# Row gathers two experts ahead, two of four turns at the beginning of a choice, and no drains on GpSimd, in an attention and mixture-of-experts kernel

## The chip, the cores and the metric

The kernel runs on one core of a Trainium2 chip. The metric is the device time of one execution in microseconds (us). TensorE (PE in the profile) multiplies matrices, VectorE (DVE) and ScalarE (ACT) work on elements, GpSimd (POOL) here issues the transfers that go by lists of rows, and SyncE (SP) issues plain transfers.

## The reference

Windowed attention over four batches of eight heads gives 3072 tokens of 512 numbers; then every token goes to one of eight experts.

```python
x = attention(q, k, v, n_global, n_local)          # (3072, 512)
logits = normed(x) @ normed(expert_emb).T / tau    # (3072, 8)
expert_idx = np.argmax(logits, axis=1)
gate_w = softmax(logits)[arange, expert_idx]
for e in range(8):
    mask = expert_idx == e
    h = np.maximum(x[mask] @ w1[e], 0.0)           # w1: (8, 512, 1024)
    out[mask] = gate_w[mask, None] * (h @ w2[e])   # w2: (8, 1024, 512)
```

## The kernel before

Up to about 200 us the kernel computes the attention, writes its rows to `x_dram` in main memory, and lists the tokens of each expert. From there on it goes through the eight experts, one after the other; the change is in this part alone.

**Rows of an expert.** Up to 512 tokens of an expert are fetched as four tiles of 128 rows. From expert 2 on each tile comes in four gathers of a quarter of a row (`gather_quarters`, gather L1030), sixteen in all, in an order that lets VectorE alone turn the tile (`turn_squares`, L1039) to have the 512 numbers of a token along the partitions. Every two gathers, a small copy on GpSimd (L1029) waits until the gathers four places before have landed, so that not too many are under way. The tiles come from a pool of eight buffers, so two experts' rows have a place.

**A choice.** The number of tokens of an expert is known only at run time. `expert` has a `tc.Switch` (L1415) with an arm for each width (256, 288, ... 512 tokens); TensorE, ScalarE and VectorE branch into the arm of that width, and out of it again. The branches are under L1825 in the profile, and the first instruction of an arm is a prefetch hint under L1415. GpSimd and SyncE have no work in the arms.

**In an arm** (`first_by_seven`) the first layer is done in seven products of half size (L1347) instead of eight, by sums of blocks: TensorE puts products into banks, VectorE adds a bank to the hidden tile (`plus`, L1357), and further products are added onto the same banks when `plus` has read them. The order is: product into x, product into y, x again, y again, v, y, v. The first `plus` reads y, ahead of the second product into y, which is the fourth of all. Between them, `fill()` lets VectorE do other small work out of the list `spare`: sums of the second layer's weights (L1090 to L1093) and of the next expert's first weights (L1115 to L1118).

**After the choice** VectorE finishes the last part of the expert before (L1165), turns the four tiles of the next expert, and sums them (`token_sums`, L1090 to L1093 on `xsum` and `xT`). In its order among them are the sums of the second layer's seven products (`Pair.begin` and `Pair.end`, L1153 on TensorE; u2 and u3 are L1158). ScalarE scales u2 (L1183) and u3 (L1190) and then p5 (L1206); TensorE's last product of the expert, added onto the bank that L1206 reads, waits for L1206.

**GpSimd's order** in the loop over experts: in iteration e it issues the gathers for expert e+1 (`prepare`), then the scatters of expert e-1's results to the output (L1300), then a drain (L1795). SyncE loads the next expert's weights: w1 in four loads of 512 KB (L169), w2 in one of 2 MB (L170), each as soon as the expert that used the buffer before is done with it. All orders on the engines are as written in the program.

Of the kernel before, what the change touches and what calls it, by code (L numbers as in the profile page):

```python
# [9 lines left out]
F32 = mybir.dt.float32  # L10
# [10 lines left out]
P = 128  # L21
NEG = 1e9
CAP = 512
# [998 lines left out]
def gather_quarters(k, ids, xgs, lo, hi):  # L1022

    src = k.x_dram[:, :].rearrange("t (b c) -> (t b) c", b=4)
    for i in range(lo, hi):
        j, g = divmod(i, 4)
        if g % 2 == 0 and i - lo > 3:
            m, h = divmod(i - 4, 4)
            k.nc.gpsimd.tensor_copy(out=k.landed[0:1, 0:2], in_=xgs[m][0:1, h * P : (h + 2) * P : P])  # L1029
        k.nc.gpsimd.indirect_dma_start(  # L1030
            out=xgs[j][:, g * P : (g + 1) * P], out_offset=None, in_=src,
            in_offset=bass.IndirectOffsetOnAxis(ap=ids[:, j, g : g + 1], axis=0),
        )
# [11 lines left out]
def new_turned(k):  # L1045
    return k.xtp.tile([P, k.NC, 2, CAP // 2], F32, name="xT", tag="xT")


def new_hidden(k):
    return k.hp.tile([P, k.NF, CAP], F32, name="hT", tag="hT")  # L1050
# [46 lines left out]
def weight_sums(k, w2):  # L1097

    b = [[w2[:, 4 * i : 4 * i + 4, j * 256 : (j + 1) * 256] for j in range(2)] for i in range(2)]
    return right_sums(k, b, k.wsum)  # L1100
# [30 lines left out]
def hidden_sums(k, a):  # L1131
    return left_sums(k, a, k.hsum)
# [255 lines left out]
def expert(k, now, coming, widths, unfinished):  # L1388


    tc = k.tc
    w1, w2 = now.w
    hT = new_hidden(k)
    if coming:
        coming.xT = new_turned(k)

    def between(f):
        for j in {5: (0,), 6: (1, 2), 7: (3,)}.get(f, ()):
            turn_row(k, coming.rows, coming.xT, j, k.nc.scalar.copy)

    a = [[hT[:, 4 * j : 4 * j + 4, i * P : (i + 1) * P] for j in range(2)] for i in range(2)]
    now.sums, spare = weight_sums(k, w2)
    left, making = hidden_sums(k, a)
    more, ahead, turns = [], [], []
    if coming:
        coming.token_sums, more = token_sums(k, coming.xT)
        if now.e:
            coming.first_sums, ahead = first_sums(k, coming.w[0])
            turns = [lambda j=j: turn_squares(k, coming.rows[2], coming.xT, j) for j in range(CAP // P)]
    spare = [[], spare[:2], spare[2:3], spare[3:], ahead[:1], ahead[1:2]]  # L1410
    tiles = range(2 if now.e else 1, CAP // P)
    ps = None if now.e else k.work0.tile([P, k.DM], F32, name="work", tag="work")
    k.order = list(range(4, 8)) + list(range(4)) if now.e else list(range(8))
    steps = widths_of(now.e)
    for arm in tc.Switch(now.width.index, len(steps), hint=now.width.hint):  # L1415
        w = steps[arm]
        if now.e:
            first_by_seven(k, now, hT, w, list(spare))
            for make in making:
                make()  # L1420
        else:
            first_by_eight(k, now.xT, w1, hT, w, between)
        for size in (32, 64):
            if w % (2 * size) >= size:
                part_in_arm(k, now, hT, w2, w // (2 * size) * 2 * size, size)
        for j in tiles:
            if j < w // P:
                second_in_arm(k, now, hT, w2, j)
        if ps:
            second(k, ps, hT, w2, range(k.NF // 2))  # L1430

    def scatters():
        for j in tiles:
            scatter_rows(k, now.y[:, j - 1, :], now.tile_ids[:, j : j + 1])
        for size in (64, 32):
            scatter_rows(k, now.y_part[size][:], now.parts[size][0], P // size)

    def choose_next():
        if coming:
            give_hint(k, coming.e, widths[coming.e])  # L1440

    out = [scatters]
    if now.e:
        pair = Pair(k, now.rows, a, left, w2, now.sums, not coming)
        choose_next()
        out += unfinished.pop()()
        number = [lambda: widths.append(take_width(k, now.e + 2))] if now.e + 2 < k.E else []
        if now.e == k.E - 2:
            number.append(lambda: load_flag(k))
        if now.e == 2:  # L1450
            ahead.append(lambda: flag_leftover(k))
        if now.e > 1:
            for make in turns:
                make()
        pair.begin(spare=(more, number, ahead[2:]) if now.e > 1 else ([], number, turns + more + ahead[2:]))
        ps = k.work0.tile([P, k.DM], F32, name="work", tag="work")
        unfinished.append(pair.end(ps[:, 0:256]))
        out.append(pair.scatter(1))
    else:
        choose_next()  # L1460
        widths.append(take_width(k, 2))
        out += unfinished.pop()()
        for make in more:
            make()
        second(k, ps, hT, w2, range(k.NF // 2, k.NF))
        unfinished.append(lambda: end_second(k, now.rows, ps))
    return out
# [172 lines left out]
def kernel(  # L1640
# [13 lines left out]
    n = Net()  # L1654
    n.tc, n.nc = tc, tc.nc
    nc = n.nc
# [24 lines left out]
    with ExitStack() as moe:  # L1681
# [40 lines left out]
        def cast(lo, hi):  # L1722
            nc.vector.tensor_copy(out=n.ids[:, lo:hi], in_=n.mt[:, lo:hi, :, 0:2])

        def prepare(e):
            t = Net()
            t.e = e
            t.y, t.y_part = ys[e % 2]
            if e < 2:
                xgs, t.gathers = gather_rows(n, n.ids[:, e], n.xgp)  # L1730
            else:
                xgs = [n.xgp.tile([P, n.DM], F32, name="xg", tag="xg") for _ in range(CAP // P)]
                gather_quarters(n, n.squares[:, e], xgs, 0, 4 if e == 2 else 16)
            t.rows = n.mt[:, e], n.ids[:, e], xgs
            if e < 2:
                t.w = n.w[e]
            else:
                t.w = new_weights(n, (wp_a, n.wp_b)[e % 2])
            return t

        with tc.manual_schedule(engines=ORDERED | set(ARMS) | {mybir.EngineType.Pool}):
# [38 lines left out]
            for e in range(n.E):  # L1780
                now, coming = coming, None
                parts_of(n, now)
                now.width = widths[e]
                if e == 1:
                    now.first_sums = first
                if e + 1 < n.E:
                    coming = prepare(e + 1)
                for scatter in pending:
                    scatter()
                if e == 1:  # L1790
                    gather_quarters(n, n.squares[:, 2], coming.rows[2], 4, 16)
                if e and coming:
                    wait_for(n, load_weights(n, e + 1, coming.w), [n.outs[-1] if e == 1 else n.out_again])

                nc.gpsimd.drain()  # L1795
                pending = expert(n, now, coming, widths, unfinished)
            for scatter in pending + unfinished.pop()():
                scatter()
# [31 lines left out]
```

## Time and profile before

| | us |
|---|---|
| median of three runs | 515.23 (513.41 to 517.9) |
| the profiled execution, its own time | 510.97 |
| its span, first to last instruction | 509.2 |
| TensorE busy | 484.6 (95%) |
| VectorE busy | 325.3 (64%) |
| ACT busy | 183.2 (36%) |
| GpSimd busy | 243.7 (48%) |

A line of the timeline has the start and the duration in us, the engine, the line of the program, the operation, what it writes and reads, how many instructions are merged into the line, and in brackets the idle time of that engine just before, with what ended it ("issue" is time for which the profile shows no reason). A q behind an engine's name means its sequencer, which handles branches, hints, drains and issues. On the time axis, expert 1's arm begins at 224, expert 2's at 257, then 307.6, 340.5, 379, 418 and 465.9 for expert 7.

### The profile page before, as it was taken

To read this page: it belongs to the slowest core of one execution; us is meant where nothing else is said; L and a number is where in the kernel's file an instruction comes from. 1 tells how busy PE (TensorE), PEld (TensorE's weight loads), DVE (VectorE), ACT (ScalarE), POOL (GpSimd) and SP (SyncE) were. 2 spreads that over 40 slices of the span, in tenths; PEclk is the share of its full clock that TensorE was granted. 3 is DMA by queue.
4 is the path that set the end of the run, shared out by engine and by line. 5 is a ranking of instruction groups with operands and counts; after the bars stand their busy time and mean duration, and the time that the engine had idled before them with its cause. 6 is when DMAs were issued, how large, how long until landed. Compare 5 with 4: busy or idle time off the path is not lost.

```text
span 509.2 us, 13692 instructions
## 1 busy us (share of the span) xinstructions
PE 484.6 (95%) x5510; PEld 399.1 (78%) x5510; DVE 325.3 (64%) x642; ACT 183.2 (36%) x445; POOL 243.7 (48%) x275
## 2 busy tenths in 40 slices
PE   7999999999999898999899999999979989999995
PEld 7677787787877687879788479789869679859964
DVE  5656677666777665848467745777656764744631
ACT  4967767858665311302112121222112111312210
POOL 4221131251453426477568575826855856854022
PEclk9999999999999999999999999999999999999999
DMA  9989999998542627529661156265354274112001
GB/s 169 195 187 189 216 240 221 201 222 208 159 106 70 180 48 179 180 79 343 203 200 41 53 200 202 75 223 181 108 188 173 54 258 163 43 70 81 0 23 68
DMA packets 112864, 76.35 MB, mean 150 GB/s; under 512 B 88517, under 2 KB 96709, under 8 KB 112721
## 3 DMA queue, kind: packets, MB, share of 16 engines
q1 hardware_dynamic: 103057, 59.00, 44.3%
q0 software_dynamic: 8064, 15.27, 9.6%
q8 instruction: 63, 1.03, 0.9%
q14 instruction: 80, 0.66, 0.4%
q10 hardware_dynamic: 1600, 0.39, 0.3%
HBM read 61.66 MB, written 17.16 MB: 155 GB/s over the span
## 4 chain that ended last, share of the span: by engine, by line
PE 71%; issue 8%; DMA 6%; POOL 6%; DVE 5%; ACT 4%; POOLq 0%; DVEq 0%; ACTq 0%
PE big L1347 22%; PE big L1153 9%; PE od L514 7%; PE work L1281 7%; PE pa L485 5%; PE pa L460 3%; DMA xg<-x_dram,squares 3%; PE work L1153 3%; PE od L524 3%; PE pa L683 2%; POOL out_dram L1300 2%; ACT ex L491 2%; PE big L1324 2%; POOL xg L1030 2%; PE work L1294 1%
## 5 line engine op out<-in xcount | busy, mean ns | idle before, releaser
L1030 POOL DMA_INDIRECT xg<-x_dram,squares x96 | 105.0, 1093 | 57.2 <-issue 42.6
L498 DVE TENSOR_TENSOR ex<-ex,table 126x768 f32<-126x768 f32 x64 | 60.7, 953 | 37.0 <-ACT ex L491 36.8
L1357 DVE TENSOR_TENSOR hT<-big,hT 128x320 f32<-128x320 f32 (+4 forms) x70 | 39.4, 565 | 56.3 <-PE big L1347 55.8
L1347 PE MATMUL big<-xT,w1t 128*128 128x160 f32 (+4 forms) x336 | 59.4, 330 | 1.6 <-issue 1.6
L491 ACT ACTIVATE ex<-pa 126x384 f32<-126x384 f32 (+1 forms) x128 | 53.2, 479 | 16.6 <-PE pa L485 15.8
L1347 PEld LDWEIGHTS big<-xT,w1t 128*128 128x128 f32 x336 | 54.8, 190 | 4.5 <-issue 2.5
L261 POOL DMA_INDIRECT meta<-mt,slot x24 | 28.5, 1187 | 41.3 <-DVE rd L558 18.2
L514 PE MATMUL od<-ex,v 126*64 126x192 f32 (+1 forms) x576 | 46.0, 305 | 0.0
L1359 ACT ACTIVATE hT<-hT 128x320 f32<-128x320 f32 (+4 forms) x42 | 22.3, 531 | 56.6 <-DVE hT L1357 56.6
L514 PEld LDWEIGHTS od<-ex,v 126*64 126x64 f32 x576 | 34.7, 136 | 7.5 <-issue 3.7
L435 POOL COPY v<-v 30x896 f32<-30x896 f32 (+1 forms) x15 | 17.2, 1158 | 47.8 <-DMA v<-in_v_dram 31.5
L1347 PE MATMUL big<-xsum,fsum 128*128 128x160 f32 (+4 forms) x224 | 39.6, 330 | 0.0
L485 PE MATMUL pa<-qT,kT 64*32 64x128 f32 (+3 forms) x2048 | 37.6, 263 | 0.3 <-DVE xs L596 0.2
L485 PEld LDWEIGHTS pa<-qT,kT 64*32 64x32 f32 (+1 forms) x2048 | 29.3, 105 | 10.8 <-issue 6.8
L1347 PEld LDWEIGHTS big<-xsum,fsum 128*128 128x128 f32 x224 | 36.4, 190 | 1.6 <-DVE fsum L1117 0.4
L1300 POOL DMA_INDIRECT out_dram<-y_arm,tids x17 | 18.8, 1106 | 36.1 <-ACT y_arm L1283 26.1
L1281 PE MATMUL work<-w2t,hT 128*128 128x512 f32 x80 | 35.1, 594 | 0.0
L1153 PE MATMUL big<-wsum,hsum 128*128 128x256 f32 x136 | 31.2, 380 | 0.5 <-DVE hsum L1117 0.4
L1153 PEld LDWEIGHTS big<-wsum,hsum 128*128 128x128 f32 x136 | 25.7, 190 | 5.1 <-issue 0.9
L1153 PE MATMUL big<-w2t,hT 128*128 128x256 f32 x112 | 27.8, 386 | 1.9 <-DVE hsum L1118 1.7
L1281 PEld LDWEIGHTS work<-w2t,hT 128*128 128x128 f32 x80 | 15.1, 190 | 17.7 <-issue 17.6
L1153 PEld LDWEIGHTS big<-w2t,hT 128*128 128x128 f32 x112 | 20.6, 190 | 9.0 <-issue 5.4
(250 smaller groups left out, 878.9 us busy)
## 6 DMA issues: line engine op xcount, KB each, us to landing
w1t<-in_moe_w_dram SPq DMA_DIRECT2D x24, 512.0 KB
w2t<-in_moe_w_dram SPq DMA_DIRECT2D x6, 2048.0 KB
v<-in_v_dram SPq DMA_DIRECT2D x32, 192.0 KB
x_dram<-xs SPq DMA_DIRECT2D x23, 256.0 KB
k<-in_k_dram SPq DMA_DIRECT2D x28, 192.0 KB
q<-in_q_dram SPq DMA_DIRECT2D x28, 192.0 KB
w1t<-in_moe_w_dram SPq DMA_DIRECT2D x32, 128.0 KB
w2t<-in_moe_w_dram SPq DMA_DIRECT2D x32, 128.0 KB
```

Of the source, the lines that this page charges most:

```text
L261: i = nc.gpsimd.indirect_dma_start(out=k.meta[:], out_offset=bass.IndirectOffsetOnAxis(ap=slot[:, t : t + 1], axis=0), in_=mt[:, t, :], in ...
L485: i = nc.tensor.matmul(u.sp[e][k0:k1, a * n + c0 : a * n + c1], lhsT=t.kT[rows, j, k0:k1], rhs=t.qT[rows, j * BLK + c0 : j * BLK + c1], st ...
L491: nc.scalar.activation(u.ex[:, e], u.sp[e][0:ROWS, 0 : 2 * u.n].rearrange("p (a c) -> p a c", a=2), AF.Exp, scale=k.scale)
L498: nc.vector.tensor_tensor(out=exv, in0=exv, in1=tab[:, :, 0 : u.n // BLK, :], op=ALU.mult)
L514: nc.tensor.matmul(g.od[a][e * D : (e + 1) * D, at : at + c1 - c0], lhsT=g.v[0:ROWS, 2 * a + e, u.j, :], rhs=u.ex[:, e, a, c0:c1], start=f ...
L1030: k.nc.gpsimd.indirect_dma_start(out=xgs[j][:, g * P : (g + 1) * P], out_offset=None, in_=src, in_offset=bass.IndirectOffsetOnAxis(ap=ids[ ...
L1153: i = self.k.nc.tensor.matmul(ps, lhsT=x[:, f, :], rhs=w[:, f, :], start=f == 0 and not add, stop=True, skip_group_check=True)
L1281: nc.tensor.matmul(ps[:], lhsT=hT[:, f, j * P : (j + 1) * P], rhs=w2[:, f, :], start=i == 0, stop=i == k.NF - 1)
L1300: i = k.nc.gpsimd.indirect_dma_start(out=k.out.rearrange("t (i m) -> (t i) m", i=n), out_offset=bass.IndirectOffsetOnAxis(ap=ids, axis=0), ...
L1347: nc.tensor.matmul(to[f // 2][:, f % 2 * 256 : f % 2 * 256 + h], lhsT=x[:, l, f * P : (f + 1) * P], rhs=y[:, l, 0:h], start=not (add or f ...
L1357: nc.vector.tensor_tensor(out=to, in0=x, in1=z, op=ALU.add)
L1359: nc.scalar.activation(to, to, AF.Relu)
```

## The change

Three things. The gathers of an expert's first two tiles (0 to 7 of sixteen) are issued one iteration earlier, behind the scatters, for experts 3 to 7; those of the last two tiles (8 to 15) stay in `prepare`. The first two turns go into the slot of `spare` at the beginning of each arm, for experts 2 to 6 (the rows are those of experts 3 to 7); the two others stay behind the choice. And the drain ahead of `expert` is gone.

```diff
@@ expert
-    spare = [[], spare[:2], spare[2:3], spare[3:], ahead[:1], ahead[1:2]]
+    early = turns[:2] if now.e > 1 else []
+    spare = [early, spare[:2], spare[2:3], spare[3:], ahead[:1], ahead[1:2]]
...
         if now.e > 1:
-            for make in turns:
+            for make in turns[2:]:
                 make()
@@ tile_lm_infinite_lambda__then__cosine_router_kernel
+        opened = {}
+
+        def rows_of(e):
+            if e not in opened:
+                opened[e] = [n.xgp.tile([P, n.DM], F32, name="xg", tag="xg") for _ in range(CAP // P)]
+            return opened[e]
+
...
-                xgs = [n.xgp.tile([P, n.DM], F32, name="xg", tag="xg") for _ in range(CAP // P)]
-                gather_quarters(n, n.squares[:, e], xgs, 0, 4 if e == 2 else 16)
+                xgs = rows_of(e)
+                gather_quarters(n, n.squares[:, e], xgs, *((0, 4) if e == 2 else (8, 16)))
...
                 if e == 1:
                     gather_quarters(n, n.squares[:, 2], coming.rows[2], 4, 16)
+                if 0 < e < n.E - 2:
+                    gather_quarters(n, n.squares[:, e + 2], rows_of(e + 2), 0, 8)
                 if e and coming:
                     wait_for(n, load_weights(n, e + 1, coming.w), [n.outs[-1] if e == 1 else n.out_again])
 
-                nc.gpsimd.drain()
                 pending = expert(n, now, coming, widths, unfinished)
```

## Rows read from the trace of the kernel before

**Rows 1.** The span and the mean granted clock of TensorE (1 is the upper of its two levels), and from the page TensorE's busy time, share and instructions.

```profile
core 0: 509.2 us, clock 0.999
PE 484.6 (95%) x5510; PEld 399.1 (78%) x5510; DVE 325.3 (64%) x642; ACT 183.2 (36%) x445; POOL 243.7 (48%) x275
```

**Rows 2.** What TensorE waited for between 220 and 510 us: us in total, number of waits, the longest.

```profile
PE work L1153 <- ACT ptmp L1206: 4.8, 2, 3.7
PE big L1153 <- DVE hsum L1118: 1.7, 1, 1.7
PE big L1347 <- issue: 1.6, 1, 1.6
```

**Rows 3.** Timeline of TensorE at the ends of experts 3 and 4.

```profile
335.70 1.89 PE L1153 MATMUL big<-w2t,hT 128*128 128x256 f32 x8
338.72 1.99 PE L1153 MATMUL work<-w2t,hsum 128*128 128x256 f32 x8 [1.13 <-ACT ptmp L1206]
...
377.13 1.99 PE L1153 MATMUL work<-w2t,hsum 128*128 128x256 f32 x8 [3.67 <-ACT ptmp L1206]
```

**Rows 4.** Timeline of VectorE behind the choices of experts 3 and 4, and of ACT at the end of expert 3.

```profile
329.89 0.48 DVE L1165 SCALAR_TENSOR_TENSOR y<-work,mts,u2g 128x256 f32<-128x256 f32 x1 [2.61 <-issue]
330.30 4.05 DVE L1039 STREAM_TRANSPOSE xT<-xg 128x512 f32<-128x512 f32 x4
...
364.73 0.48 DVE L1165 SCALAR_TENSOR_TENSOR y<-work,mts,u2g 128x256 f32<-128x256 f32 x1 [2.96 <-issue]
365.13 3.06 DVE L1039 STREAM_TRANSPOSE xT<-xg 128x512 f32<-128x512 f32 x3
371.66 1.10 DVE L1039 STREAM_TRANSPOSE xT<-xg 128x512 f32<-128x512 f32 x1 [3.47 <-DMA xg<-x_dram,squares]
...
338.21 0.45 ACT L1206 ACTIVATE ptmp<-work,mts 128x256 f32<-128x256 f32 x1
```

**Rows 5.** GpSimd: the first gathers of the rows of experts 5 and 6 in the timeline, and the drain ahead of the former (duration in ns, minimum, median and maximum, and the start in us).

```profile
L1795 POOLq DRAIN  x1: 18532/18532/18532, 321.3 to 321.3; - x1
...
340.76 1.31 POOL L1030 DMA_INDIRECT xg<-x_dram,squares  x1 [8.77 <-issue]
...
378.15 1.08 POOL L1030 DMA_INDIRECT xg<-x_dram,squares  x1 [3.61 <-issue]
```

**Rows 6.** GpSimd: the first and the eighth gather of expert 3's rows, and the eighth and the sixteenth of expert 6's.

```profile
250.29 0.94 POOL L1030 DMA_INDIRECT xg<-x_dram,squares  x1 [3.57 <-PE big L1153]
...
262.90 0.94 POOL L1030 DMA_INDIRECT xg<-x_dram,squares  x1 [0.30 <-issue]
...
392.74 1.94 POOL L1030 DMA_INDIRECT xg<-x_dram,squares  x1 [0.30 <-issue]
...
404.71 0.94 POOL L1030 DMA_INDIRECT xg<-x_dram,squares  x1 [0.30 <-issue]
```

**Rows 7.** VectorE: the last sum of expert 2's results, and the turns of expert 6's rows behind the choice of expert 5.

```profile
306.88 0.42 DVE L1158 TENSOR_TENSOR y<-ptmp 128x256 f32<-128x256 f32 x1
...
404.63 4.04 DVE L1039 STREAM_TRANSPOSE xT<-xg 128x512 f32<-128x512 f32 x4
```

**Rows 8.** All gathers of quarters: their number and time on GpSimd (ns, minimum, median, maximum) and the time from issue to landing; then the median time to landing (last number, us) of those issued from 256 to 268 us and from 400 to 420 us.

```profile
L1030 POOL DMA_INDIRECT xg<-x_dram,squares x96: 942/975/1939, 208.6 to 444.6; - x96
DMA to landing us min/median/max: 2.4/3.2/7.6
xg<-x_dram,squares POOLq DMA_INDIRECT x6, 6.0
xg<-x_dram,squares POOLq DMA_INDIRECT x6, 3.0
```

**Rows 9.** The entries of experts 3 and 4: VectorE's branch and the hint behind it (ns; start in us), its first sum in the arm, and TensorE's fourth product of expert 4.

```profile
L1825 DVEq COMPARE_BRANCH  x1: 65/65/65, 307.0 to 307.0; - x1
L1415 DVEq BRANCH_PREFETCH_HINT  x1: 45/45/45, 307.6 to 307.6; - x1
311.12 0.49 DVE L1357 TENSOR_TENSOR hT<-big,hT 128x320 f32<-128x320 f32 x1 [3.83 <-PE big L1347]
...
L1825 DVEq COMPARE_BRANCH  x1: 59/59/59, 340.2 to 340.2; - x1
L1415 DVEq BRANCH_PREFETCH_HINT  x1: 45/45/45, 343.3 to 343.3; - x1
344.40 0.52 DVE L1357 TENSOR_TENSOR hT<-big,hT 128x352 f32<-128x352 f32 x1 [2.85 <-PE big L1347]
347.71 2.55 PE L1347 MATMUL big<-xsum,fsum 128*128 128x176 f32 x16
```

**Rows 10.** The entry of expert 2: SyncE's load of w2, VectorE's branch and hint, its first sums (two instructions of 0.69 us, merged), TensorE's fourth product, and the busy times from 258.4 to 265.7 us (the last two numbers are the DMA engines' busy share and GB/s).

```profile
257.11 0.38 SPq L170 DMA_DIRECT2D w2t<-in_moe_w_dram  x1
L1825 DVEq COMPARE_BRANCH  x1: 59/59/59, 260.8 to 260.8; - x1
L1415 DVEq BRANCH_PREFETCH_HINT  x1: 45/45/45, 266.4 to 266.4; - x1
266.55 1.29 DVE L1357 TENSOR_TENSOR hT<-big,hT 128x512 f32<-128x512 f32 x2 [4.47 <-PE big L1347]
267.56 3.62 PE L1347 MATMUL big<-xsum,fsum 128*128 128x256 f32 x16
258.40:265.70 7.30, 7.28 (x34) 6.08 (x33) 3.62 (x5) 1.17 (x2) 4.85 (x6) 1.00 0.97 317
```

## The prediction

> **What bounds the kernel now.** I read the shares of the page first, then the list of what TensorE waited for, then for each of those waits the stretch of every engine around it. TensorE is busy 95% of the span, and the clock stands at its upper level throughout [rows 1]. So a time can only come out of the places where TensorE has nothing to do, or be put there. From 220 us to the end of the experts there are 8.1 us of them, but for one of 0.2 [rows 2]: 4.8 us in two waits for ACT's L1206, 1.7 us for hsum (expert 1, which the change doesn't touch) and 1.6 us of "issue" at the entry of expert 6's choice. That is the whole stock.
>
> The two waits for L1206 stand at the ends of experts 3 and 4, 1.13 us and 3.67 us [rows 3]. Both have the same chain behind them. L1206 is quick, but in ACT's order it stands behind L1190, and L1190 needs VectorE's u3 (L1158), and in VectorE's order u3 stands behind four turns of the next expert's rows and four sums of them [rows 4]. In expert 3 no turn waits: VectorE leaves the choice at 329.89, turns for 4.05 us without a gap, and the chain is late by its own length. In expert 4 it is late for another reason as well: the fourth turn waits 3.47 us for a gather [rows 4].
>
> Why that gather was late is seen on GpSimd [rows 5]. The first gather of expert 5's rows began at 340.76 after 8.77 us in which GpSimd had nothing to do; the drain that stands in front of it began at 321.3, lasted 18.53 us and ended at 339.87. So here a drain holds the queue 7.9 us after the last scatter, at 331.99. Ahead of the next gathers, at 378.15, the gap is 3.61 us. Sixteen gathers then follow each other, and the last has landed at 371.6, while VectorE wants its rows at 368.2, when the third turn is done.
>
> **The change part by part.**
>
> *Drains.* Eight are removed. Nothing in VectorE, ACT or TensorE waits for one; they hold only GpSimd's queue, where gathers and scatters stand behind them, 3.6 to 8.8 us of idle time each in the stages of the experts [rows 5, 6]. On the path this is worth something only through the gathers, and is counted there, not again.
>
> *Gathers 0 to 7, two experts ahead.* None is added: 96 at about 0.97 us before and after, with two landing copies fewer in each expert from 3 on. A block of eight takes 13.6 us where it ran freely (250.29 to 263.84) and 16.5 us where the copies waited longest (378.15 to 394.68) [rows 5, 6]. New order on GpSimd in expert e: gathers 8 to 15 of e+1, scatters of e-1, gathers 0 to 7 of e+2. For expert 5's rows: the last scatter of expert 2 needs VectorE's L1158 at 306.88 to 307.30 [rows 7]; so the first eight begin at about 309 and end by 325, the other eight end by 342 at the worst rate, and with the longest landing seen, 7.6 us [rows 8], all is there by 350. They are wanted from 364 on. The wait of 3.47 us goes with some 14 us to spare. The scatters have eight gathers in front of them instead of sixteen and come out earlier; nobody on the path waits for one. GpSimd also gets ahead for experts 6 and 7 (their first eight start once the scatters of experts 3 and 4 are out, at about 341 and 377 in the old times, over 30 us ahead of need).
>
> *Two turns moved out of the end of an expert.* They cost 2 x 1.03 us = 2.05 us of VectorE (a fourth of 4.05, [rows 4]) and stand no longer ahead of u3. Expert 3: L1206 would run at about 336.2 and TensorE finishes the product ahead of its wait at 337.6; the wait of 1.13 us goes. Expert 4: without the landing wait (3.47) and two turns (2.05), u3 comes 5.5 us earlier; TensorE's wait was 3.67, so it goes too. What is late next there is TensorE's own chain of products. Gain: 1.13 + 3.67 = 4.8 us.
>
> *Two turns put at the beginning of a choice (experts 2 to 6).* What hides them is VectorE's idle time ahead of its first sum of products (L1357): 3.83 us in expert 3 and 2.85 in expert 4 [rows 9]. But the trace puts that down to TensorE as the last releaser, and VectorE isn't free for all of it: after its branch at 340.2 the first instruction of the arm, the prefetch hint, runs at 343.3 [rows 9], 3.0 us later. So in expert 4 the turns fit only partly into the gap; they push the first sum by about 1 us. The point at which this hurts is TensorE's fourth product, which adds onto the banks that the first sum reads. In expert 4 the chain (entry at 343.3, two turns, one sum of 0.52) ends at 345.9, and the fourth product begins at 347.7 [rows 9], all in old times: nothing lost, with 1.8 us left. In expert 3 the entry is at 307.6, so the turns end at 309.7, before the first sum's old time of 311.12: nothing moves. Experts 5 and 6 have entries like expert 4's and wider products, so more is left.
>
> Expert 2 does not. There VectorE's branch ran at 260.8 and its first instruction of the arm at 266.4, 5.6 us later [rows 10], while the 2 MB load of w2t issued at 257.11 kept the DMA engines 97% busy [rows 10]. The first sum ran at once, at 266.55, and TensorE's fourth product began at 267.56 with nothing to spare. With two turns ahead of it (266.45 to 268.5) and 0.69 us for its first half, the banks come free at 269.2: TensorE waits 1.7 us that it doesn't wait now. Bounds: 0, if the entry takes 3.0 us as in expert 4 or 0.5 us as in expert 3 (branch 307.0, hint 307.6 [rows 9]); 2.4 us, if the second tile's last gather lands late. For that: the first eight gathers of expert 3 start at about 247.0 instead of 250.29 (of the gap of 3.57 us, 0.3 stays [rows 6]), end at 260.6, and land between 263.0 and 268.2 by the shortest and the longest landing, 2.4 and 7.6 us [rows 8], counted from the last issue's end to be on the safe side. VectorE wants the second tile at 267.5. I take 1.7, because entry and load stand in the same order after the change.
>
> Here a rule of the skill speaks against the change. The Trainium skill, Runtime: NRT & Kernel Launch, section Instruction fetch mechanics, says that a taken branch to a place outside the two instruction pages at hand has to wait for a DMA fetch of that page. The rows agree for the entries of 3.0 and 5.6 us; the entry of 0.5 us would be a page already there. By that rule longer arms (two turns with their waits in each of nine) can move any entry from one kind to the other, and it cannot be told beforehand which; expert 2's term would then be 0 or 1.7 as the pages fall.
>
> *What stays.* TensorE's 1.64 us at the entry of expert 6's choice: its program is the same, so I keep it (bounds 0 and 1.64 gained). The weights' loads on SP are not moved. The end, from the last product to the end of the program, is not touched.
>
> *Sum.* -1.13 - 3.67 + 1.7 = -3.1 us. On the profiled execution, 510.97 us with a span of 509.2 [rows 1], that gives 507.9. The median of the runs is 515.23, 4.3 us above the profiled one, and no row shows where those lie. I keep them as they are: 515.23 - 3.1 = 512.1 us.
>
> **The rivals.**
>
> *No wait in expert 2.* VectorE's entry takes 3.0 us or less, and the gathers have landed. For it: the other entries shown are shorter than 5.6 [rows 9]. Against it: the load that stood in its way is still issued at the same place. Then -4.8 us, 510.4.
>
> *The longer runs wait longer for gathers.* In expert 5 the turns ran without a wait, but the last gather had ended on GpSimd at 405.65 and the fourth turn began at about 407.6 [rows 6, 7]: the margin is about nothing. If landings or drains are slower by a few microseconds, as the 7.87 us in expert 4's case shows that they can be, the wait of expert 4 grows one for one, and expert 5 gets one of its own. The 4.3 us between median and profile may be of this kind. Then the change takes them too: 3.1 to 4.8 + up to 4.3, about 7 us, 508.2. Against it: that the excess is there is known, its place is not.
>
> *The change doesn't do what it says.* The rows are there early, but another thing in front of u3 (the exit of the choice, 2.61 and 2.96 us of "issue" [rows 4]) grows, or the drain's time comes back as slower issues. Then only the 1.13 us or nothing is won: 514.5.
>
> *Slower: the head of a choice waits for a gather.* Until now a late gather met VectorE at the end of an expert; now it meets it before the first sum, with the fourth product behind it at once. In expert 2 the second tile may be late: if its last gather lands at L, TensorE waits L + 1.03 + 0.69 - 267.56. That eats the whole 4.8 us from L = 270.6 on, 10 us after the last issue; beyond the longest landing of 7.6 us. Were L 273 (two of those landings), it would be 7.2 us lost, and the run 2.4 us slower: 517.6. For it speaks that the gathers meet the 2 MB load of w2t there: beside it six landed in a median of 6.0 us, where six others, mostly without it, took 3.0 [rows 8]. The Trainium skill, DMA: Bandwidth & Descriptors, section Issuing engines are not separate DMA queues, says that transfers of all issuers run interleaved on the same 16 engines; by that an earlier start only moves the gathers into the load. The trace agrees in that doubling.
>
> **How the numbers follow.** Forecast 512.1: 0.38. No wait in expert 2, 510.4: 0.22. Longer runs, 508.2: 0.22. Nothing of it, 514.5: 0.10. Slower, 517.6: 0.08. The range of 8 in 10 reaches from 507 (the third case, with some more of the 1.64) to 515.5 (the fourth). A difference of 1%, 5.2 us, is about what a measurement of this kernel can tell from none. Faster by more needs under 510.1: the third case and half of the second, and a little of the first, 0.36. Slower by over 1%, above 520.4: 0.04. Within: 0.60.
>
> **What would show it.** Right, if no turn (L1039) waits for a gather at the end of expert 4, TensorE no longer waits for L1206, and GpSimd's gathers follow its scatters at 0.3 us. Expert 2: turns behind the hint at about 266.4, the first sum at 268.5 and a wait of TensorE of about 1.7 us before its fourth product. Wrong, if VectorE's entries or exits of the choices are of other lengths, if TensorE gets "issue" at other entries, or if the 4.3 us turn out to be gather waits.

## The result and the profile after

The changed kernel took 515.41 us in the median of 20 runs (512.22 to 520.89), the kernel before 514.12 us (20 runs, 508.72 to 521.89). The ratio is 1.0082, with a 95% interval of 1.0055 to 1.0109: 0.8% slower, where 3.1 us less had been forecast. A ratio, here and below, leaves out the slow runs, those over 1.5% above the fastest of their kernel, and is not that of the two medians, which is 1.0025 here. A second comparison gave 1.0078 (1.0037 to 1.0119). Both intervals lie above 1; the size is known to some microseconds only. The profiled execution took 517.69 us with a span of 515.9.

First the page's span, the granted clock, and what TensorE waited for between 220 and 510 us (total in us, number, longest).

```profile
span 515.9 us, 13665 instructions
...
core 0: 515.9 us, clock 0.987
...
PE big L1347 <- DVE hT L1357: 1.7, 1, 1.7
PE big L1347 <- issue: 1.2, 1, 1.2
PE big L1153 <- DVE hsum L1118: 1.2, 1, 1.2
```

Against [rows 2], both waits for L1206 are gone, and one of 1.7 us for VectorE's hT is new. That is what the change was to do, and the next fence shows it in the timeline: the last products of experts 3 and 4 without the waits of [rows 3], the entry of expert 2 with its early turns, and GpSimd, where expert 5's gathers now follow the scatters after 0.30 us instead of the 8.77 of [rows 5].

```profile
344.49 1.99 PE L1153 MATMUL work<-w2t,hsum 128*128 128x256 f32 x8
...
379.07 1.89 PE L1153 MATMUL work<-w2t,hsum 128*128 128x256 f32 x8
...
272.13 2.07 DVE L1039 STREAM_TRANSPOSE xT<-xg 128x512 f32<-128x512 f32 x2 [4.59 <-DMA xg<-x_dram,squares]
274.11 1.26 DVE L1357 TENSOR_TENSOR hT<-big,hT 128x512 f32<-128x512 f32 x2
274.82 3.72 PE L1347 MATMUL big<-xsum,fsum 128*128 128x256 f32 x16 [1.67 <-DVE hT L1357]
...
322.66 0.98 POOL L1300 DMA_INDIRECT out_dram<-y,idss  x1 [0.30 <-DVE wsum L1091]
323.94 0.99 POOL L1030 DMA_INDIRECT xg<-x_dram,squares  x1 [0.30 <-issue]
...
350.69 0.94 POOL L1030 DMA_INDIRECT xg<-x_dram,squares  x1 [0.30 <-issue]
```

The loss is behind the last product. The first pair of lines is the kernel before (L1825 is the end of the program there; durations in ns, minimum, median, maximum; starts of the first and the last), with its last scatter; the others are the changed kernel's (the end is L1834).

```profile
L1825 POOLq DRAIN  x3: 50/103/1033, 507.0 to 509.0; - x3
504.22 0.98 POOL L1300 DMA_INDIRECT out_dram<-y,idss  x1 [2.03 <-DVE y L1165]
```

```profile
505.63 0.98 POOL L1300 DMA_INDIRECT out_dram<-y,idss  x1 [2.03 <-DVE y L1165]
L1834 POOLq DRAIN  x3: 46/103/6283, 508.8 to 515.6; - x3
L1834 ACTq DRAIN  x2: 8/8/8, 504.1 to 515.3; - x2
L1834 PEldq DRAIN  x2: 8/8/8, 505.8 to 515.4; - x2
...
510.00:515.90 5.90, 0.00 (x0) 0.00 (x0) 0.00 (x0) 0.00 (x0) 0.00 (x0) 0.50 0.00 0
```

Both programs end with a drain on every engine. GpSimd's took 1.03 us before and takes 6.28 now; the others' second drains, 8 ns long, stand behind it at 515.3. In the last 5.9 us no engine and no transfer is busy (the zeros; 0.50 is the granted clock, the lower level). So these are no transfers that land late: the drain itself is long. The last packet of GpSimd's own DMA queue ended at 508.4, and the drain began at 508.8. From the last scatter's issue to the end of the program it was 5.0 us and is 10.3.

The balance in three stretches, cut at the first product of expert 0 (L1324) and at the start of the last L1153. The lines give the first and the last start of each, before and then after.

```profile
L1324 PE MATMUL big<-xT,w1t x64: 299/299/374, 200.8 to 210.8; 128*128 128x160 f32 x64
L1153 PE MATMUL work<-w2t,hsum x56: 379/379/483, 255.2 to 503.0; 128*128 128x256 f32 x56
```

```profile
L1324 PE MATMUL big<-xT,w1t x64: 298/299/374, 206.5 to 216.5; 128*128 128x160 f32 x64
L1153 PE MATMUL work<-w2t,hsum x56: 379/379/483, 260.6 to 504.4; 128*128 128x256 f32 x56
```

In the table, "drain" is the longest at the program's end; the lines below the first two are runs told of in the next section.

| kernel | up to the experts | experts | from the last product on | waits for L1206 | wait for hT | drain |
|---|---|---|---|---|---|---|
| before, profiled | 200.8 | 302.2 | 6.2 | 4.8 | 0 | 1.03 |
| changed, profiled | 206.5 | 297.9 | 11.4 | 0 | 1.7 | 6.28 |
| before, e17 | 203.4 | 299.3 | 6.1 | 2.2 | 0 | 0.81 |
| changed, e9 | 206.0 | 297.0 | 11.0 | 0 | 1.7 | 6.28 |
| only the drains out, e2 | 207.0 | 298.3 | 11.3 | 1.2 | 0 | 6.28 |
| changed, with all drains, e3 | 203.8 | 303.2 | 6.0 | 0 | 4.4 | 0.63 |
| changed, one drain, e1 | 203.8 | 298.0 | 5.9 | 0 | 1.7 | 0.63 |
| one drain, no early turns, e12 | 203.3 | 298.4 | 6.1 | 1.3 | 0 | 0.80 |
| one drain, early turns from expert 3, e18 | 201.8 | 295.7 | 6.1 | 0 | 0 | 0.63 |

The experts gained 4.3 us and the end lost 5.2. The first column, in which the code is the same, differs by 5.7 us in the profiled pair. In the changed kernel's execution the clock was granted at the lower level for a part of these 20 us of the attention, in the other (the first two lines) it was not (the column before the last two). Means of 0.86 and 0.80 are 6.8 us at the lower of the two levels, so by an estimate at most 3.4 us of the 5.7; the rest isn't placed, and 200.8 and 203.4 in the table stand at the same mean clock, 0.999.

```profile
140.00:150.00 10.00, 9.44 (x291) 7.60 (x282) 7.18 (x25) 6.31 (x17) 6.55 (x6) 1.00 0.44 108
150.00:160.00 10.00, 8.79 (x198) 6.13 (x200) 8.06 (x29) 4.78 (x15) 4.44 (x4) 1.00 0.24 68
```

```profile
140.00:150.00 10.00, 7.09 (x136) 5.75 (x134) 7.36 (x25) 4.21 (x12) 3.79 (x4) 0.86 0.24 66
150.00:160.00 10.00, 10.00 (x223) 7.28 (x219) 5.39 (x23) 4.02 (x11) 3.52 (x4) 0.80 0.38 74
```

### The profile page after: what moved, and what is told of

Read it like the earlier page. It is cut to its first block, busy times and chain, and to the rows that moved or that the text cites. A ratio compares the mean times of both kernels' runs of the same rounds, so it can differ in the third digit from the quotient of the medians.

```text
span 515.9 us, 13665 instructions
## 1 busy us (share of the span) xinstructions
PE 488.5 (95%) x5510; PEld 402.5 (78%) x5510; DVE 326.2 (63%) x642; ACT 184.0 (36%) x445; POOL 236.6 (46%) x265
## 3 DMA queue, kind: packets, MB, share of 16 engines
q8 instruction: 63, 1.03, 0.9%
## 4 chain that ended last, share of the span: by engine, by line
PE 55%; issue 2%; DVE 1%; DMA 1%; POOL 1%; POOLq 0%
PE big L1347 25%; PE big L1153 12%; PE work L1281 7%; PE work L1153 4%; PE work L1294 3%; PE big L1324 2%; PE work L1072 1%; DMA xg<-x_dram,idss 1%; POOL out_dram L1300 1%; PE work L1062 0%; DVE w1t L1116 0%; DVE xT L1039 0%; DVE hsum L1117 0%; DVE hsum L1118 0%; DVE hT L1357 0%
## 5 line engine op out<-in xcount | busy, mean ns | idle before, releaser
L514 PE MATMUL od<-ex,v 126*64 126x192 f32 (+1 forms) x576 | 47.9, 313 | 0.0
L261 POOL DMA_INDIRECT meta<-mt,slot x24 | 27.3, 1139 | 43.7 <-DVE xs L596 13.1
L435 POOL COPY v<-v 30x896 f32<-30x896 f32 (+1 forms) x15 | 15.5, 1045 | 52.2 <-DMA v<-in_v_dram 30.1
L485 PE MATMUL pa<-qT,kT 64*32 64x128 f32 (+3 forms) x2048 | 38.8, 272 | 0.2
L485 PEld LDWEIGHTS pa<-qT,kT 64*32 64x32 f32 (+1 forms) x2048 | 30.4, 108 | 10.7 <-issue 7.8
L1039 DVE STREAM_TRANSPOSE xT<-xg 128x512 f32<-128x512 f32 x24 | 24.9, 1081 | 13.3 <-issue 6.7
L1153 PE MATMUL big<-wsum,hsum 128*128 128x256 f32 x136 | 31.2, 380 | 0.7 <-DVE hsum L1117 0.4
L1153 PEld LDWEIGHTS big<-wsum,hsum 128*128 128x128 f32 x136 | 25.7, 190 | 5.3 <-issue 1.1
L1153 PE MATMUL big<-w2t,hT 128*128 128x256 f32 x112 | 27.6, 386 | 1.2 <-DVE hsum L1118 1.2
```

The lines of the kernel that those rows point to most:

```text
L261: i = nc.gpsimd.indirect_dma_start(out=k.meta[:], out_offset=bass.IndirectOffsetOnAxis(ap=slot[:, t : t + 1], axis=0), in_=mt[:, t, :], in ...
L485: i = nc.tensor.matmul(u.sp[e][k0:k1, a * n + c0 : a * n + c1], lhsT=t.kT[rows, j, k0:k1], rhs=t.qT[rows, j * BLK + c0 : j * BLK + c1], st ...
L514: nc.tensor.matmul(g.od[a][e * D : (e + 1) * D, at : at + c1 - c0], lhsT=g.v[0:ROWS, 2 * a + e, u.j, :], rhs=u.ex[:, e, a, c0:c1], start=f ...
L1039: k.nc.vector.transpose(out=xT[:, :, :, j * half : (j + 1) * half].rearrange("p c a (g i) -> p g c a i", i=LACE), in_=xgs[j][:].rearrange( ...
L1153: i = self.k.nc.tensor.matmul(ps, lhsT=x[:, f, :], rhs=w[:, f, :], start=f == 0 and not add, stop=True, skip_group_check=True)
```

## The experiments

The theory to be tested (A) was that a drain works through the transfers that GpSimd has issued since the drain before, landed or not; without the eight drains the one at the end does it for all, where nothing covers it. While e5 to e8 and e13 to e16 ran, the kernel before itself took 530.6 and 529.2 us in the median, with engines standing still inside the arms; times of these two groups are read only against the kernel before in the same group, and single executions of them only for the rows of their drains and waits.

**One drain back, ahead of expert 7 (e1).**

```diff
+                if e == n.E - 1:
+                    nc.gpsimd.drain()
                 pending = expert(n, now, coming, widths, unfinished)
```

> The changed kernel with one drain put back, ahead of the last expert (7); the other seven stay out. Theory A, a drain's work grows with the transfers that GpSimd has issued since the last drain, and the changed kernel pays all of it in the drain at the end of the program (6.28 us, 1.03 before): here the drain at the end is back at about 1.0 us, the one ahead of expert 7 takes 6 us or more at a place where GpSimd has nothing to do for 25 us, and the time is 5 us under the changed kernel, some 1 to 5 us under the kernel before. Theory B, the long drain at the end waits for something else (late scatters, the branch at the end): it stays at 6 us and the time is that of the changed kernel.

Measured: 509.67 us (12 runs) against 513.49 for the kernel before; ratio 0.9953 (0.9917 to 0.9989). A single drain for which nobody waits takes 5.65 of the 6.28 us away and leaves the experts as they were (298.0 against 297.9). The line has GpSimd's drains at the end.

```profile
L1836 POOLq DRAIN  x3: 46/103/633, 506.2 to 507.4; - x3
```

**The kernel before, only its drains out (e2).**

```diff
-                nc.gpsimd.drain()
                 pending = expert(n, now, coming, widths, unfinished)
```

> The kernel before without its eight drains; gathers and turns as before. Theory A: the drain at the end of the program takes about 6.3 us instead of 1.0; the gathers of expert 5's rows start 8 us earlier, so expert 4's turn no longer waits for a gather and TensorE's wait there falls from 3.7 to about 1 us (the chain of four turns is left, as in expert 3). Sum: 5.3 lost, some 2.6 won, so 2 to 5 us above the kernel before. Theory B: no longer drain at the end, 2 to 3 us under the kernel before.

Measured: 515.39 us, ratio 1.0039 (1.0 to 1.0077). The end is that of the changed kernel to the nanosecond:

```profile
L1824 POOLq DRAIN  x3: 46/103/6283, 509.5 to 516.3; - x3
PE work L1153 <- ACT ptmp L1206: 1.2, 1, 1.2
```

So the loss at the end belongs to the removed drains alone. The second line (waits from 220 us on) says that a good part of the gain does too: in this execution expert 4's wait is gone with the gathers at their old place, and only expert 3's 1.2 us are left for the other two parts.

**The change with all its drains (e3).**

```diff
+                nc.gpsimd.drain()
                 pending = expert(n, now, coming, widths, unfinished)
```

> The changed kernel with all eight drains put back: early gathers and early turns alone. Theory A: the drain at the end takes 1.0 us, TensorE's waits for ACT's L1206 stay gone, the wait of 1.7 us in expert 2's arm stays or grows (the first eight gathers of expert 3 start 3 us later no more than before, the drain comes behind them), time 2 to 4 us under the kernel before. If the early turns themselves were what costs, it would be at the changed kernel's time or above.

Measured: 515.41 us, ratio 1.0055 (1.0011 to 1.0099). The end is short (0.63), and the loss is now in the experts, 303.2 us: with the drains in the queue the second early turn of experts 5 and 6 waits for its gathers at the head of the choice. In expert 5 TensorE's fourth product waits with it, in expert 6 it did not. Its 2.7 us are half of the 5.3 by which this part is longer than the changed kernel's; TensorE's other waits come to 0.7 more, and the rest isn't placed.

```profile
387.75 1.08 DVE L1039 STREAM_TRANSPOSE xT<-xg 128x512 f32<-128x512 f32 x1 [6.65 <-DMA xg<-x_dram,squares]
389.32 4.43 PE L1347 MATMUL big<-xsum,fsum 128*128 128x192 f32 x16 [2.70 <-DVE hT L1357]
...
430.18 1.11 DVE L1039 STREAM_TRANSPOSE xT<-xg 128x512 f32<-128x512 f32 x1 [7.65 <-DMA xg<-x_dram,squares]
```

**The one drain at other places: ahead of expert 4 (e4), 5 (e8) and 2 (e15).** The edit is shown against e1; what stands behind the # is for the other two runs.

```diff
-                if e == n.E - 1:
+                if e == 4:              # e8: e == n.E - 3; e15: e == 2
```

> The changed kernel with one drain ahead of expert 4. GpSimd issues 49 transfers after it, against 7 after the last drain of the kernel before and some 180 in all. Theory A, the work grows with their number: the drain at the end takes between 1.7 and 2.5 us, in a line between 1.0 and 6.3. Rival: any drain at all, or none, decides: 1.0 or 6.3 us.

> The changed kernel with its one drain ahead of expert 5 instead of expert 7: 27 indirect transfers of GpSimd come behind it, between 7 (drain at the end 0.63 us) and 49 (4.07 us). Theory A (the drain at the end pays for each transfer since the last drain, 0.082 us each by those two): 2.3 us at the end (2.0 to 2.6). Theory B (the drain costs a step once more than some ten transfers are out): 3.5 to 4.1 us. Time by A about 511.3, by B about 512.7, both within 2 us for the clock.

> The changed kernel with its one drain ahead of expert 2: 93 indirect transfers come behind it. The drains at the end measured so far are 0.63 us for 7 transfers, 2.27 for 27, 4.07 for 49 and 6.28 for all. Theory A with a limit (0.082 us a transfer up to some 76, and no more beyond): 6.28, the same as with no drain. Rival (it goes on rising by 0.082 us and the 6.28 is set by something else, such as transfers that were retired by a wait earlier on): 7.7 us.

Measured, in this order (one execution each, of 512.07, 552.12 and 552.77 us, the last two out of the two groups named above):

```profile
L1836 POOLq DRAIN  x3: 46/103/4067, 505.4 to 510.0; - x3
```

```profile
L1836 POOLq DRAIN  x3: 46/103/2271, 547.2 to 550.0; - x3
```

```profile
L1836 POOLq DRAIN  x3: 46/103/7661, 542.6 to 550.8; - x3
```

With 7, 27, 49 and 93 transfers behind the last drain, the end takes 0.633, 2.271, 4.067 and 7.661 us: a straight line of 0.082 us a transfer, (7.661 - 0.633) / 86. The expectation for e4 was wrong by a factor of about two, because I had laid the line through 6.28 us for all 182. That the line goes on past 6.28 was the rival in e15, and it won: the 6.28 is no upper limit. So theory A holds for up to 93 transfers behind a drain; for all 182 it would give about 14.9 us, and that part of it fails.

**The changed kernel, e1 and two variants beside each other (e9 to e12).** e11 is e1 with early turns from expert 3 on alone; e12 is e1 with none. The edit is shown against e1.

```diff
-    early = turns[:2] if now.e > 1 else []
+    early = turns[:2] if now.e > 2 else []       # e12: early = []
...
-            for make in turns[2:]:
+            for make in turns[len(early):]:
```

> The changed kernel itself, timed beside the three below and the kernel before on one chip, since the second group of runs was 17 us slower for the kernel before too. Theory (the experts part gains 4 to 5 us, the end loses 5.3, whatever the chip): within 2 us of the kernel before, drain at the end 6.28. Rival (more gathers in flight at the choices delay the engines' code loads on a chip where these are slow): 5 to 15 us slower than the kernel before where that kernel takes 525 or more, and within 2 us where it takes 515 or less.

> The changed kernel with one drain ahead of expert 7, again. Theory: 4 to 6 us below the changed kernel of the same call, and 3.5 to 5 below the kernel before, drain at the end 0.63. Rival (late code loads, as above): still some 5 us below the changed kernel, but above the kernel before by up to 10 us where that kernel takes 525 or more.

> One drain ahead of expert 7, and early turns from expert 3 on alone, again beside the kernel that it is to be compared with. Theory: 1.0 to 1.7 us below the kernel with the drain ahead of expert 7. Rival: the same within 1 us, another wait in expert 2 having come up in L1153 or at its second product.

> One drain ahead of expert 7, and all turns behind the choices, again beside the kernel that it is to be compared with. Theory (early turns are worth nothing in sum once the drains are out): within 1.2 us of the kernel with the drain ahead of expert 7, with a wait for L1206 of 1.1 to 1.3 in expert 3 in place of the 1.7 in L1347 of expert 2. Rival: 3 us or more slower than that kernel, with waits for L1206 of 3 to 5 us in sum.

Measured against 511.17 us for the kernel before: the changed kernel 515.79 (1.0078); one drain 509.61, ratio 0.9939 (0.9896 to 0.9982); early turns from expert 3 on 506.49, ratio 0.9878 (0.9805 to 0.995); no early turns 509.57, ratio 0.989 (0.9805 to 0.9976). The changed kernel and e1 differ by 6.2 us here and by 5.7 between the first two comparisons, of which the drain at the end is 5.65. (By the medians the last three lie 1.6, 4.7 and 1.6 us under the kernel before.) The early turns of expert 2 cost what they were priced at: without them the 1.7 us are gone and the first sum stands directly ahead of a fourth product that doesn't wait. The two lines are e18's, below; e11 has the same.

```profile
267.18 1.29 DVE L1357 TENSOR_TENSOR hT<-big,hT 128x512 f32<-128x512 f32 x2 [4.46 <-PE big L1347]
...
268.18 3.62 PE L1347 MATMUL big<-xsum,fsum 128*128 128x256 f32 x16
```

Those of the later experts are worth more than I expected. From e12 to e18 and e11 the experts part falls by 2.6 and 3.5 us (298.4 to 295.7 and 294.9). Waits that I can name make up 2.2 of it: 1.3 for L1206 in expert 3, 0.5 of "issue" in L1153, and 1.6 against 1.2 at the entry of expert 6. So in e1 the gain of the late experts and the loss of expert 2 about cancel, which fits that e1 and e12 take the same time.

**The same variants beside a kernel before of 530.6 us (e5, e7), and the first of them again (e16, e18).**

> The changed kernel with a drain ahead of expert 7 alone, and in expert 2 all four tiles turned behind the choice as in the kernel before; experts 3 to 7 turn two at the head of the choice. Theory (the early turns of expert 2 meet a late load of the arm's instructions or a late gather and hold VectorE's first plus): the wait of 1.7 us of TensorE for VectorE's hT in L1347 of expert 2 goes, no wait for L1206 comes back there, since the kernel before has none in expert 2, and the time falls by 1.0 to 1.7 us below that of the kernel with the drain ahead of expert 7, so to about 508 (506.5 to 509.5). Rival (the wait goes over to a later place, as it does when VectorE's two turns of 1.0 us each stand between the choice and the first sums): the wait in L1347 goes but one of 1 to 1.7 us for L1206 or hsum appears in expert 2, and the time is that of the kernel with the drain alone, 509.7. The end is short in both: drain at the end 0.6 us.

> The changed kernel with a drain ahead of expert 7 alone, and no early turns: the eight gathers go two experts ahead, the drains ahead of experts 0 to 6 are out, and all four tiles are turned behind the choice. It tells the worth of the early turns from that of the gathers and drains. Theory: without early turns expert 3's wait for L1206 comes back at 1.1 to 1.2 us (it stood also where only the drains were out) and the 1.7 us in L1347 of expert 2 goes, so that the early turns are worth nothing in sum: 509 to 510, the same as with the drain alone. Rival (the early turns are what gained in experts 3 and 4): waits for L1206 of 3 to 5 us in sum come back and the time is 512 to 514.

> One drain ahead of expert 7 and early turns from expert 3 on, timed once more for its interval. Theory: 506.5 to 508, 1.0 to 1.4% below the kernel before, no wait in L1347 of expert 2, an experts part of 295 us. Rival: it stands with the kernel with the drain alone at 509.6, and 506.5 was a matter of five runs with an undisturbed clock.

> One drain ahead of expert 7 and early turns from expert 3 on, beside the kernel before. Theory: 1.0 to 1.4% below the kernel before where that takes 511 to 515 us, as in its run of 506.5 us. If code loads come late again (the kernel before at 525 or more), it is 0 to 1.5% slower than that kernel, as in its two groups there, since with no drains GpSimd's gathers stand closer to those loads.

Measured: e5 543.41 and e7 538.63 us against 530.6, ratios 1.0009 (0.9926 to 1.0091) and 1.0153 (1.0073 to 1.0234); e16 536.0 against 529.23, without a ratio; e18 507.19 us (11 runs) against 514.58, ratio 0.9916 (0.9874 to 0.9958). Where the kernel before takes 511 to 515 us, this kernel (e11, e18) is 0.8 to 1.2% below it. That it is also below e1's was seen beside it once: 3.1 us in the medians of e11 and e10, with runs that overlap. In the other two groups no gain shows, and nothing about a microsecond in expert 2 could be read there. One line of what stood still there: ACT in an arm of expert 4 in e7, and the same place in the kernel before in e6.

```profile
ACT y L1296 <- remote: 15.3, 1, 15.3
```

```profile
ACT y L1296 <- remote: 6.2, 1, 6.2
```

My expectations call this late loads of code, e13's as if it were known. No row shows that it is. In e7 the queues that the profile marks "instruction" moved two packets beside this wait, both ended by 375.0, and ACT went on at 388.7. What it is stays open.

**The kernel before, profiled again (e6, e13, e14, e17).**

> The kernel before once more, one look, to learn whether the wait of 3.67 us in expert 4 with a drain that ends 7.9 us behind the last transfer is what an ordinary execution of it shows. Theory: waits for L1206 of 4 to 5.5 us in sum in experts 3 and 4, drain at the end 0.6 to 1.1 us, a span of 509 to 513 by the clock. Rival (the long drain of expert 4 was one execution's): waits for L1206 of 1 to 2.5 us in sum, and the gain to be had in the experts part is the smaller by 2 to 3 us.

> The kernel before, another look, since the one that fell into the second group was taken while code loads came late for every kernel. Theory (its two waits for L1206 are ordinary): 4 to 5.5 us in sum in experts 3 and 4, an experts part of 301 to 303 us from the first L1324 to the last product, drain at the end 0.6 to 1.1. Rival (the 3.67 us of expert 4 was one execution's): 1 to 2.5 us in sum and an experts part of 298.5 to 300.5, which would explain why the kernel with one drain is only 2 to 4 us below it in the medians where the profiles differ by 4.5.

> The kernel before, a second look, with the same two cases: waits for L1206 of 4 to 5.5 us in sum and an experts part of 301 to 303, or 1 to 2.5 and 298.5 to 300.5.

> The kernel before, one more look, for its waits on a chip whose code loads come in time. Theory: waits for L1206 of 4 to 5.5 us in sum and an experts part of 301 to 303 us. Rival, which the two looks with late code loads speak for (6.7 us in three waits in one, 1.6 in one wait in the other): the wait of expert 3 stands at 1.1 to 1.6, that of expert 4 comes only where its drain ends some 7.5 us behind its last transfer, and the part is 298.5 to 300.5.

Measured: e6, e13 and e14 (532.17, 521.48, 519.26 us) are of the two groups named above; waits for L1206 of 1.9, 6.7 and 1.6 us, between others that the profile of before doesn't have. e17 (510.63 us) has the clock of the first profile, 0.999: 2.2 us in sum, an experts part of 299.3. The drain that stands in front of the gathers of expert 5's rows is long there too (16.3 us, 18.5 in [rows 5]), but the four turns run without a gap, and TensorE waits 0.86 us where it waited 3.67 [rows 3, 4].

```profile
368.05 4.04 DVE L1039 STREAM_TRANSPOSE xT<-xg 128x512 f32<-128x512 f32 x4
...
341.00 1.99 PE L1153 MATMUL work<-w2t,hsum 128*128 128x256 f32 x8 [1.38 <-ACT ptmp L1206]
...
376.61 1.99 PE L1153 MATMUL work<-w2t,hsum 128*128 128x256 f32 x8 [0.86 <-ACT ptmp L1206]
```

## Why the prediction was wrong

*The step that failed* is two sentences: that nothing waits for a drain and its worth is "counted there, not again", and that "the end, from the last product to the end of the program, is not touched". The program's own end is a drain of GpSimd, and it does a part of the work that the eight had done beside the products. That is 5.25 us on the path (1.03 to 6.28), more than everything the change could gain. A hint of it stood in the trace of before: the program ends with a drain, which took 1.03 us with 7 transfers behind the eighth. I didn't ask what work a drain does, nor who would do it when it is gone. Its price did not stand there, and the 7.9 us of [rows 5] are not it: most of them were a wait for landings. The last two scatters there are the line below (median time to landing of those whose landing is known, 7.7 us), GpSimd's queue moved packets until 338.4, and the drain ended about 1.4 us later, where 22 transfers at 0.082 us would be 1.8.

```profile
out_dram<-y,idss POOLq DMA_INDIRECT x2, 7.7
```

The rival *The change doesn't do what it says* came nearest: it named the drain's time as coming back, but as slower issues, and these follow at 0.30 us. That 515.41 lies within the stated range, 507 to 515.5, is luck: that bound stood for a gain that fails, not for an end that grows.

*A term that was perhaps mis-sized:* expert 4's wait. 3.67 us is what one execution showed; another showed 0.86, with its gathers in time. By e17 the two waits are worth 2.2 us instead of 4.8. The experts part then gains 299.3 - 297.5 = 1.8 us (297.5 is the mean of the changed kernel's two), the end loses about 5.2, and the sum of +3.4 lies inside the interval of the ratio, 2.8 to 5.6 us of 514. With the first profile it would be about +0.9. The five profiles of the kernel before have 4.8, 2.2, 1.9, 6.7 and 1.6 us, so the prediction took one value of a wait that varies.

*Right:* where the stock lies, and that L1206's waits go. Expert 2's new wait: 1.7 us forecast, 1.67 measured, with the hint 5.7 us behind the branch (5.6 before) and the turns right behind it. The same row names a gather as what ended VectorE's wait, but in all five arms of the changed kernel that have early turns, and in e9's and e1's, the first turn starts 0.26 us behind the hint; so the entry held it, and no gather. The rule of the Trainium skill that the prediction names (Runtime: NRT & Kernel Launch, section Instruction fetch mechanics) would have allowed 0 as well; the long entry stayed where it was.

*A sign of being wrong that came:* an entry of another length. Expert 3's was 0.5 us before; in the changed kernel VectorE's branch ran at 314.0 and its hint at 317.2, 3.2 us later. In the twelve profiles in which expert 2 has no early turns it is 0.5, in the eight with them 3.2 to 6.0 us, so it goes with them: an entry moved from one kind to the other, as the prediction had said that longer arms can do, in the arm where it didn't expect it. TensorE didn't wait there in the changed kernel, so "nothing moves" held for TensorE, not for VectorE.

*Right as well, the gathers:* the sixteen of expert 5 are issued by 351.6 and wanted from 370.5 on. The first eight began some 7 us later than I had reckoned, since the gathers in front of them held the queue until 315.8, with 3.5 us of waiting for a landing; nothing came of it. The entry of expert 6 kept 1.2 of 1.64 us.

*With one drain put back the sum holds.* -3.1 us were forecast; e1 and e10 stand at 0.9953 and 0.9939 of the kernel before, 2.4 and 3.1 us less (3.8 and 1.6 by the medians of all runs). That agreement owes something to chance: by e17 expert 4's term was too large, and the late experts' early turns, which I priced at nothing beyond it, gave something back.

*The 4.3 us between median and profiled execution*, from which I made a rival (longer runs wait longer for gathers, 508.2), go with the clock. In the profiled execution it was 0.999; 50 further runs of the kernel before, in two groups, had 0.984 to 0.999, 0.992 in the mean, and those with a lower clock are the longer, as 518.3 us at 0.987 and 508.4 at 0.997. By a straight line through each group 0.01 of the clock goes with 7 to 8 us, so the 0.007 between 0.999 and 0.992 with 5 to 6, by estimate, which leaves nothing for gather waits to explain. The long runs weren't profiled, so that they have none isn't shown. The rival *Slower: the head of a choice waits for a gather* put its loss at the wrong place: such a gather did cost 2.7 us in e3, in expert 5, with the drains still in the queue.

## What to carry to other kernels

Before an instruction that "nobody waits for" is taken out, ask what work it does and where the next instruction of its kind stands: if that is the program's end, work moves from under cover onto the path. One such instruction late, in a gap of its engine, kept the gain here. And before a single wait of a profile is priced, read a second execution: its size may vary where its place does not.

## What the runs showed of the hardware

At the program's end a drain on GpSimd took 0.082 us for each indirect transfer that GpSimd had issued since its last drain, although all had landed: 0.633 us for 7, 2.271 for 27, 4.067 for 49, 7.661 for 93. (Where GpSimd's queue still moved packets when the drain began, or until just then, the 7 took up to 1.03 us.) A drain in the middle of the program waits for landings as well: in the kernel before those ahead of experts 2 to 6, with 22 transfers each, ended 1.3 to 1.5 us after the queue's last packet, and 2.7 to 7.8 us after the last issue. The three lines are the single drains ahead of an expert in e15, e8 and e1.

```profile
L1806 POOLq DRAIN  x1: 9862/9862/9862, 299.1 to 299.1; - x1
```

```profile
L1806 POOLq DRAIN  x1: 6467/6467/6467, 425.6 to 425.6; - x1
```

```profile
L1806 POOLq DRAIN  x1: 6933/6933/6933, 463.7 to 463.7; - x1
```

Counted from the end of the last issue on GpSimd, which each outlasts, they are 7.35 us for 89 transfers (on the line: 7.33), but 4.08 for 155 and 5.72 for 175, and the 6.28 at the end stand for 182 (two of them plain): each time the line for 106 transfers fewer. e4's, ahead of expert 4, doesn't fit: 6.55 us for 133, where 27 would be 2.27; there the queue moved packets until 373.9, 1.6 us before the drain ended. What settles the first 106 wasn't tried. The Trainium skill, VectorE: DVE Perf Modes, section The DRAIN you can't avoid, says of the runtime's own drains that "those are ~12 ns constant" and stand on all five engines; the trace agrees for ACT and TensorE at the end (8 ns) and not for GpSimd (46 and 103 ns, and the long one of 633 to 7661 ns; whether that one is the runtime's own no row shows).
